# Sliding-window attention and a SwiGLU block on one core: two projection products trade places, two VectorE additions get precedence, and the last block's sums are held back

## The chip, the cores and the metric

The kernel runs on one core of a Trainium2 chip. The metric is device time in microseconds (us), the median of several runs; the kernel before takes 342.95 us (4 runs, 342.94 to 343.35). The core's engines work side by side and each takes its own instructions in a fixed order: TensorE (PE; its weight loads are listed as PEld), VectorE (DVE), ScalarE (ACT), GpSimd (POOL) and SyncE (SP). POOL, SP and ACT also issue transfers (DMA). An engine waits for another through semaphores.

## What is computed

The reference, cut to what matters:

```python
# attention: 8 batches, 8 heads, 576 tokens, head size 64, window 128, ALiBi bias
scores = scale * np.matmul(q, k.transpose(0, 1, 3, 2))
scores = np.where(mask, scores + bias[None], -1000000000.0)
attn = np.exp(scores - max); attn = attn / sum
x = (attn @ v) as 4608 tokens x 512
# SwiGLU block: d_model 512, d_ff 1536
g = x @ w_gate
silu = g * (1.0 / (1.0 + np.exp(-g)))
val = x @ w_val
out = (silu * val) @ w_out          # 4608 x 512, float32
```

## The kernel before

**Tiling.** The 4608 tokens are 9 blocks of 512 (n = 0 to 8). Attention is done in 36 units that produce `xT`, the transposed input of a block. The two wide products (gate and value) of a block produce `hT[n]`, 12 row tiles of 128 x 512. The last product (projection with `wo_sb`) turns `hT[n]` into output rows. The gate, value and projection work of one block runs beside the attention of later blocks and the projection of the block before: the code is generators, and `ffn()` and `everything()` decide which one is advanced next.

**The projection in seven products.** From block 1 on, the projection of a block is Strassen's scheme in Winograd's form: `strassen(n, t)` (line 507) runs for t = 0 and t = 1, each in seven steps of six 128x256 matmuls. Each step ends with a `yield`. X and Y are the two accumulators in PSUM. In the code's order the steps are:

1. X = A11 B11; ACT copies X (`p1s`) or, for blocks 5 to 7, seeds `p2` with it (lines 543 to 547)
2. p2 += A12 B21; DVE writes the top left output (`osb`, line 551 or 540)
3. X += S2 T2 (the "sixth" product); ACT copies X to `u2s` (line 558)
4. Y = S1 T1 (the "fifth" product); ACT copies Y to `p5s` (line 564), or DVE does for the last block's t = 1 (line 562)
5. X += S3 T3; DVE writes low right = X + `p5s` (line 540 through `half_plus`)
6. Y += S4 B22; DVE writes top right = Y + `u2s` (line 540)
7. X += A22 T4; low left (line 577 on DVE for the last block, else 579 on ACT)

For all blocks but the last, X and Y are halves of one PSUM tile, that is of one bank. For the last block (`end`) they are two tiles of the pool `ps_a`, two banks. S1 is made in place in `hT`, S2, S3 and S4 in three buffers, by four DVE instructions for every two row tiles (`four_sums`): S3 (line 488), S1 (489), S2 (490), S4 (491). S2 needs S1, S4 needs S2.

**Gate and value of the last three blocks in seven products.** For n = 6, 7 and 8 `gate_val_by_seven(n)` (line 615) does the gate and value products of a pair of row tiles u (0 to 5) in seven steps of four 128x256 matmuls, `first` to `seventh`. `third` adds on DVE v1 = Y + u2 (line 663) and multiplies it into `hT` (664); `seventh` adds v2 = X + p5 (line 670); `fourth` accumulates into X, which v2 has read, and its result goes through ACT (678) and DVE (679) into `hT`. `seven_steps()` interleaves two pairs: first(u), seventh(u-1), fifth(u), sixth(u), fourth(u-1), second(u), third(u), so that step number k of a block is 7u plus the place in this list. After every third step one step of `strassen(n-1, ...)` is put in.

**What sets the order.** From step 60 of the main loop on (which takes in all steps of the Strassen projection), PE's instructions stand in the order in which the code issues them (`manual_schedule` for PE alone). DVE and ACT instructions, ACT's transfers among them, are placed by the scheduler, by its own estimate of when they are ready and by their priority; `tc.high_priority()` raises the latter. Small DVE instructions that are not due yet are collected in `later`, and one or two of them are issued after a step.

**The end.** Block 8 has nothing after it. Step 1 of t = 0 is put in at k = 41; behind the last gate and value product come the other 13 steps of both halves, in the order t = 1, 0, 1, 0, 0, 0, 1, 0, 0, 1, 1, 1, 1 (line 780). So the steps at the end are, as t.step: 0.1, 1.1, 0.2, 1.2, 0.3, 0.4, 0.5, 1.3, 0.6, 0.7, 1.4, 1.5, 1.6, 1.7. The last block's outputs are stored in pieces by SP and ACT (`store(..., two)`, line 446).

Of the kernel before, what the change touches and what calls it, by code (L numbers as in the profile page):

```python
# [51 lines left out]
def kernel(  # L52
# [10 lines left out]
    nc = tc.nc  # L63
# [6 lines left out]
    NBLK = NTOK // 512  # L70
# [396 lines left out]
    T1, T2, T3, T4 = (consts.tile([P, HM, HC], FP16, name=f"T{n}") for n in (1, 2, 3, 4))  # L467
# [25 lines left out]
    def at_once(fs):  # L493
        for f in fs:
            f()
# [11 lines left out]
    def strassen(n, t):  # L507

        h = hT[n]
        A11, A12 = h[:, 0:HM, 0:256], h[:, HM:NMB, 0:256]  # L510
        S1, A22 = h[:, 0:HM, 256:512], h[:, HM:NMB, 256:512]
        S2, S3, S4 = hsum[n]
        cols = slice(t * P, (t + 1) * P)
        end = n == NBLK - 1
        seeded = SEVEN_FROM <= n + 1 < NBLK
        factor = 1.0 if n >= SEVEN_FROM else 0.5
        if end:
            X, Y = (ps_a.tile([P, HC], FP32, name="po", tag="a", bufs=4) for _ in range(2))
            p2 = ps_f.tile([P, HC], FP32, name="p2", tag="gv")
        else:  # L520
            po = ps_f.tile([P, 2, HC], FP32, name="po", tag="po", bufs=1)
            X, Y = po[:, 0, :], po[:, 1, :]
            p2 = (ps_f.tile([P, HC], FP32, name="p2", tag="gv") if seeded
                  else ps_a.tile([P, HC], FP32, name="p2", tag="a"))
        top, low = (opool.tile([P, DM], FP32, name="osb", tag="osb") for _ in range(2))
        if end and t:
            spare = [opool.tile([P, DM], FP32, name="osb", tag="osb") for _ in range(2)]
            p1s, p5s, u2s = spare[0][:, 0:HC], spare[0][:, HC:DM], spare[1][:, 0:HC]
        else:
            p1s, p5s, u2s = (supool.tile([P, HC], FP32, name=i, tag=i, bufs=1)  # L530
                             for i in ("p1s", "p5s", "u2s"))

        def product(dst, a, b, start=False):
            for m in range(HM):
                nc.tensor.matmul(dst, a[:, m, cols], b[:, m, :], start=(start and m == 0),  # L535
                                 stop=(m == HM - 1), skip_group_check=True)

        def half_plus(dst, a, b):
            with tc.high_priority() if n + 1 < SEVEN_FROM else ExitStack():
                nc.vector.scalar_tensor_tensor(out=dst, in0=a, scalar=factor, in1=b,  # L540
                                               op0=ALU.mult, op1=ALU.add)

        product(X, A11, B11, True)
        if seeded:
            nc.scalar.copy(p2, X)
        else:
            nc.scalar.mul(p1s, X, factor)
        yield
        product(p2, A12, B21, not seeded)
        if seeded:  # L550
            nc.vector.tensor_scalar_mul(top[:, 0:HC], p2, factor)
        else:
            half_plus(top[:, 0:HC], p2, p1s)
        if end and t:
            store(n, t, top, 0, HC)
        yield
        product(X, S2, T2)
        nc.scalar.mul(u2s, X, factor)
        yield
        product(Y, S1, T1, end)  # L560
        if end and t:
            nc.vector.tensor_scalar_mul(p5s, Y, factor)
        else:
            nc.scalar.mul(p5s, Y, factor)
        yield
        product(X, S3, T3)
        half_plus(low[:, HC:DM], X, p5s)
        if end and t:
            store(n, t + 2, low, HC, DM, True)
        yield  # L570
        product(Y, S4, B22)
        half_plus(top[:, HC:DM], Y, u2s)
        store(n, t, top, HC if end and t else 0, DM, end)
        yield
        product(X, A22, T4)
        if end:
            nc.vector.tensor_scalar_mul(low[:, 0:HC], X, factor)
        else:
            nc.scalar.mul(low[:, 0:HC], X, factor)
        store(n, t + 2, low, 0, HC if end and t else DM, end)  # L580
        yield
# [33 lines left out]
    def gate_val_by_seven(n):  # L615

        x = xT[n]
        A11, A12 = x[:, 0:HK, 0:256], x[:, HK:NKB, 0:256]
        S1, A22 = x[:, 0:HK, 256:512], x[:, HK:NKB, 256:512]
        S2, S3, S4 = xsum.pop(n)  # L620
        hT[n] = hpool.tile([P, NMB, 512], FP16, name="hT", tag="hT")
        live = {}

        def product(dst, w, c0, a, start=False):
            for i in range(2):
                for kb in range(HK):
                    nc.tensor.matmul(dst[:, i, :], w[:, kb, c0 + i * P:c0 + (i + 1) * P], a[:, kb, :],  # L627
                                     start=(start and i == 0 and kb == 0),
                                     stop=(i == 1 and kb == HK - 1), skip_group_check=True)

        def first(u):
            X, Y = (ps_a.tile([P, 2, 256], FP32, name=i, tag="a", bufs=4) for i in ("gX", "gY"))
            Z = ps_f.tile([P, 2, 256], FP32, name="gZ", tag="gv")
            live[u] = X, Y, Z
            product(X, G1, 2 * u * P, A11, True)
            nc.scalar.copy(Z, X)

        def fifth(u):
            Y = live[u][1]
            product(Y, tsum[u][0], 0, S1, True)  # L640
            p5 = epool.tile([P, 2, 256], FP32, name="p5", tag="exc", bufs=5)
            nc.scalar.copy(p5, Y)
            live[u] += (p5,)

        def second(u):
            Z = live[u][2]
            product(Z, G2, 2 * u * P, A12)
            s = supool.tile([P, 2, 256], FP16, name="s1", tag="tt")
            nc.scalar.activation(s, Z, AF.Silu)
            live[u] += (s,)  # L650

        def sixth(u):
            X = live[u][0]
            product(X, tsum[u][1], 0, S2)
            u2 = epool.tile([P, 2, 256], FP32, name="u2", tag="exc", bufs=5)
            nc.scalar.copy(u2, X)
            live[u] += (u2,)

        def third(u):
            X, Y, Z, p5, u2, s = live[u][:6]  # L660
            product(Y, V2, 2 * u * P, S4)
            v_ = supool.tile([P, 2, 256], FP16, name="v1", tag="uu")
            nc.vector.tensor_add(v_, Y, u2)
            nc.vector.tensor_mul(hT[n][:, 2 * u:2 * u + 2, 0:256], s, v_)

        def seventh(u):
            X, Y, Z, p5, u2, s = live[u]
            product(X, tsum[u][2], 0, S3)
            v_ = supool.tile([P, 2, 256], FP16, name="v2", tag="uu")
            nc.vector.tensor_add(v_, X, p5)  # L670
            live[u] += (v_,)

        def fourth(u):
            X, v_ = live[u][0], live[u][-1]
            del live[u]
            product(X, tsum[u][3], 0, A22)
            s = supool.tile([P, 2, 256], FP16, name="s2", tag="tt")
            nc.scalar.activation(s, X, AF.Silu)  # L678
            nc.vector.tensor_mul(hT[n][:, 2 * u:2 * u + 2, 256:512], s, v_)  # L679

        return {f.__name__: f for f in (first, second, third, fourth, fifth, sixth, seventh)}
# [23 lines left out]
    def ffn():  # L705
# [44 lines left out]
        for n, k, name, which in seven_steps():  # L750
            if k == 0 and n > SEVEN_FROM:
                assert next(parts, 0) == 0
                parts = chain(strassen(n - 1, 0), strassen(n - 1, 1))
            if n == SEVEN_FROM and k in (1, 3, 10, 17):
                later.extend(gate_val_weight_sums(2 + (k + 4) // 7))
            yield 0.5
            if k % 3 == 2 and k < 42:
                next(parts)
                yield 0.75
            if k == 20 and n + 1 < NBLK:  # L760
                later.extend(x_sums(n + 1))
            if k == 35:
                later.extend(sums(n, 0))
            if name == "fourth" and which is not None and which[1] > 3:
                if which == (NBLK - 1, 5):
                    at_once(final)
                else:
                    later.extend(sums(which[0], which[1] - 3))
            if n == NBLK - 1 and k == 40:
                final = sums(n, 2)  # L770
                later.append(final.pop(0))
            for _ in range(2 if len(later) > 4 or k >= 39 or k < 7 else 1):
                if later:
                    later.pop(0)()
            if n == NBLK - 1 and k == 41:
                next(ends[0])
                yield 0.75
# [235 lines left out]
```

The softmax here doesn't subtract the row's maximum and nothing guards it: scores larger than these inputs give would overflow.

## Time and profile before

| | |
|---|---|
| median of 4 runs | 342.95 us |
| the profiled execution's own time | 343.14 us |
| its span, first to last instruction | 341.3 us |
| PE busy / DVE / ACT | 329.8 / 277.3 / 207.0 us |
| mean granted TensorE clock | 0.998 |

DVE's busy time by stretch (the windows view, 40 us each): 34.6 us in 40 to 80, 33.3 in 80 to 120, 36.0 in 120 to 160, 37.9 in 160 to 200, 39.9 in 200 to 240; then 12.9 in 240 to 260, 15.7 in 260 to 280 and 13.8 in 280 to 300 (20 us each). Blocks 6 to 8 with their seven products begin at about 244 us; the last gate and value product ends at about 327.8 us, the last matmul at about 337.1 us.

How to read a line of the timeline: start, duration, engine, line of the kernel, operation, output tile <- input tiles, size, count of merged instructions, and in brackets the idle time before it with what ended it. The tile names are the program's without buffer numbers: `po` is X or Y of the projection, `T` is one of T1 to T4, `S` one of S2 to S4, and `po<-T,hT` is a product with S1 or A22, which lie in `hT`. A PE row's duration holds the passage through the array; from the start of one 128x256 matmul to the next it is 0.109 us.

### The profile page before, as it was taken

How to read it: one execution, taken by the hardware profiler on the slowest of the kernel's cores; microseconds unless marked ns; L12 is line 12 of the kernel's file. 1: busy time of each engine (PE TensorE's matmuls, PEld its weight loads, DVE VectorE, ACT ScalarE, POOL GpSimd, SP SyncE). 2: the span in 40 equal slices, each digit the busy share in tenths (PEclk: the TensorE clock that was granted, in tenths of full speed). 3: DMA queues.
4: the chain of work that ended last, by engine and by line, in shares of the span. 5: the costliest groups of instructions: out<-in, count | busy, mean ns of one | idle time of the engine just before them, and what ended most of it. 6: DMA issues, size and time to landing. Idle time of an engine off the chain costs nothing.

```text
span 341.3 us, 7787 instructions
## 1 busy us (share of the span) xinstructions
PE 329.8 (97%) x2983; PEld 218.5 (64%) x2983; DVE 277.3 (81%) x652; ACT 207.0 (61%) x412; POOL 109.6 (32%) x136
## 2 busy tenths in 40 slices
PE   7999989999999999999999999999999999999994
PEld 4484445444456566566655655665788878888884
DVE  6577886999798779998899999999855975775683
ACT  3758676465766675656655557463477667676640
POOL 8968672548865175834017000000000000000000
PEclk9999999999999999999999999999999999999999
DMA  9999999899999999999969922041101101011014
GB/s 154 170 180 175 164 170 151 79 140 160 160 172 140 172 155 158 164 158 140 200 130 101 179 33 79 15 85 27 61 16 48 63 0 64 24 40 63 0 71 116
DMA packets 160037, 37.37 MB, mean 109 GB/s; under 512 B 147328, under 2 KB 155648, under 8 KB 160000
## 3 DMA queue, kind: packets, MB, share of 16 engines
q0 software_dynamic: 118336, 18.62, 82.3%
q1 hardware_dynamic: 40976, 17.64, 28.7%
q10 hardware_dynamic: 688, 0.62, 0.6%
q8 instruction: 23, 0.38, 0.5%
q14 instruction: 14, 0.11, 0.1%
HBM read 37.91 MB, written 9.44 MB: 139 GB/s over the span
## 4 chain that ended last, share of the span: by engine, by line
PE 75%; DVE 14%; ACT 6%; issue 2%; DMA 1%; ACTq 0%; DVEq 0%
PE po L535 16%; PE pg L400 14%; PE pv L400 14%; PE gX L627 8%; PE av L348 4%; PE gY L627 4%; PE ps L280 3%; PE po L454 2%; PE p L535 2%; DVE hT L430 2%; PE gZ L627 2%; ACT tt L418 2%; ACT ex L286 2%; DVE uu L419 2%; PE px L374 1%
## 5 line engine op out<-in xcount | busy, mean ns | idle before, releaser
L400 PE MATMUL pv<-xT,wv_sb 128*128 128x512 f16 (+2 forms) x320 | 76.5, 358 | 0.6 <-DVE uu L419 0.3
L400 PE MATMUL pg<-xT,wg_sb 128*128 128x512 f16 (+2 forms) x320 | 75.8, 358 | 0.3 <-DVE xT L376 0.2
L418 ACT ACTIVATE tt<-pg 128x512 f16<-128x512 f32 (+2 forms) x70 | 41.3, 590 | 47.7 <-PE pg L400 46.6
L286 ACT ACTIVATE ex<-ps 128x512 f16<-128x512 f32 x96 | 50.0, 606 | 9.9 <-PE ps L280 9.9
L419 DVE SCALAR_TENSOR_TENSOR uu<-tt,pg 128x512 f16<-128x512 f16 (+2 forms) x69 | 46.0, 667 | 10.5 <-ACT tt L418 10.2
L430 DVE TENSOR_TENSOR hT<-uu,pv 128x512 f16<-128x512 f16 (+2 forms) x70 | 46.7, 667 | 3.0 <-PE pv L400 1.3
L185 POOL DMA_DIRECT2D va<-in_v_dram x40 | 34.4, 863 | 36.9 <-PE av L348 28.8
L400 PEld LDWEIGHTS <-wv_sb 128*128 128x128 f16 x320 | 28.3, 98 | 25.1 <-issue 3.2
L535 PEld LDWEIGHTS <-hT 128*128 128x128 f16 x384 | 37.0, 98 | 10.6 <-issue 0.8
L400 PEld LDWEIGHTS <-wg_sb 128*128 128x128 f16 x320 | 28.2, 98 | 23.3 <-issue 2.6
L191 POOL DMA_DIRECT2D kn<-in_k_dram x39 | 33.3, 858 | 19.8 <-DMA kT<-kn 10.7
L191 POOL DMA_DIRECT2D qn<-in_q_dram x39 | 33.5, 865 | 16.0 <-DMA va<-in_v_dram 8.2
L535 PEld LDWEIGHTS <-S 128*128 128x128 f16 x288 | 27.3, 98 | 9.0 <-issue 1.4
L292 DVE TENSOR_TENSOR ex<-ex,m_reg 128x1024 f16<-128x1024 f16 x42 | 28.8, 687 | 3.0 <-ACT ex L286 3.0
L351 DVE TENSOR_TENSOR x<-av,rec 128x256 f16<-128x256 f32 x72 | 28.8, 420 | 0.4
L535 PE MATMUL po<-T,S 128*128 128x256 f16 x192 | 26.5, 273 | 0.6 <-DVE S L490 0.3
L535 PE MATMUL po<-T,hT 128*128 128x256 f16 x192 | 26.0, 273 | 0.1
L679 DVE TENSOR_TENSOR hT<-s,v 128x512 f16<-128x512 f16 x18 | 7.6, 424 | 18.5 <-ACT s L678 18.5
L320 ACT ACTIVATE exc<-psc 128x512 f16<-128x512 f32 x40 | 21.3, 609 | 1.9 <-PE psc L316 1.9
L348 PEld LDWEIGHTS <-ex 128*128 128x128 f16 x384 | 17.4, 97 | 4.6 <-issue 1.3
L348 PE MATMUL av<-va,ex 128*128 128x65 f16 x384 | 19.3, 193 | 0.7 <-ACT ex L286 0.7
L280 PE MATMUL ps<-qT,kT 64*128 64x256 f16 x192 | 16.7, 272 | 0.4 <-DVE qT L223 0.2
(134 smaller groups left out, 537.5 us busy)
## 6 DMA issues: line engine op xcount, KB each, us to landing
out_dram<-osb SPq DMA_DIRECT2D x32, 256.0 KB, 2.5
va<-in_v_dram POOLq DMA_DIRECT2D x32, 128.0 KB, 7.9
qn<-in_q_dram POOLq DMA_DIRECT2D x31, 128.0 KB, 8.7
kn<-in_k_dram POOLq DMA_DIRECT2D x31, 128.0 KB, 8.1
wg_sb<-in_moe_w_gate_dram POOLq DMA_DIRECT2D x6, 256.0 KB, 7.6
wv_sb<-in_moe_w_val_dram POOLq DMA_DIRECT2D x6, 256.0 KB, 8.1
wo_sb<-in_moe_w_out_dram POOLq DMA_DIRECT2D x2, 768.0 KB, 9.3
kn<-in_k_dram POOLq DMA_DIRECT2D x8, 64.0 KB, 7.4
```

Source lines behind the costliest of these rows:

```text
L185: nc.gpsimd.dma_start(va[rank][p0:p1, :, 0:D], src)
L191: nc.gpsimd.dma_start(t_[p0:p1], src)
L286: nc.scalar.activation(e[:, o:o + 2, :], banks[q4][par], AF.Exp, scale=scale)
L292: nc.vector.tensor_mul(e[:, o, :], e[:, o, :], reg[:, o, :])
L348: nc.tensor.matmul(av[:, j, :], w, val, start=(n == 0), stop=(n == len(todo) - 1))
L351: nc.vector.tensor_mul(x[:, 4 * half:4 * half + 4, :], av[:, :, 0:D], rec.broadcast_to([P, 4, D]))
L400: nc.tensor.matmul(ps[:, c0:c1], w[:, kb, ms], xT[n][:, kb, c0:c1], start=(kb == 0 and c0 == 0), stop=(kb == NKB - 1 and c1 == 512), skip_ ...
L418: nc.scalar.activation(tt, pg[:, c0:c1], AF.Tanh, scale=0.5)
L419: nc.vector.scalar_tensor_tensor(out=uu, in0=tt, scalar=one if (n, m) == PIN else 1.0, in1=pg[:, c0:c1], op0=ALU.add, op1=ALU.mult)
L430: nc.vector.tensor_mul(hT[n][:, m, c0:c1], acted[(n, m)][1][:, c0:c1], pv[:, c0:c1])
L535: nc.tensor.matmul(dst, a[:, m, cols], b[:, m, :], start=(start and m == 0), stop=(m == HM - 1), skip_group_check=True)
L627: nc.tensor.matmul(dst[:, i, :], w[:, kb, c0 + i * P:c0 + (i + 1) * P], a[:, kb, :], start=(start and i == 0 and kb == 0), stop=(i == 1 an ...
```

## The change

1. In `strassen`, the steps 3 and 4 trade places: first Y = S1 T1 with `p5s`, then X += S2 T2 with `u2s`. The order of t at the end (line 780) stays.
2. In `third` and `seventh` of the gate and value products, the additions v1 and v2 are issued with high priority.
3. In `ffn`, the single instruction of the last sums (S3 of block 8's last pair), which is appended to `later` at k = 40, isn't taken out at k = 40 and 41, nor is what else lies in `later`; at the last `fourth` all that is left in `later` is issued ahead of `final`.

```diff
@@ strassen(n, t)
-        product(X, S2, T2)
-        nc.scalar.mul(u2s, X, factor)
-        yield
         product(Y, S1, T1, end)
         if end and t:
             nc.vector.tensor_scalar_mul(p5s, Y, factor)
         else:
             nc.scalar.mul(p5s, Y, factor)
+        yield
+        product(X, S2, T2)
+        nc.scalar.mul(u2s, X, factor)
         yield
         product(X, S3, T3)
@@ gate_val_by_seven(n)
         def third(u):
...
-            nc.vector.tensor_add(v_, Y, u2)
+            with tc.high_priority():
+                nc.vector.tensor_add(v_, Y, u2)
...
         def seventh(u):
...
-            nc.vector.tensor_add(v_, X, p5)
+            with tc.high_priority():
+                nc.vector.tensor_add(v_, X, p5)
@@ ffn()
                 if which == (NBLK - 1, 5):
-                    at_once(final)
+                    at_once(later + final)
+                    later.clear()
...
             for _ in range(2 if len(later) > 4 or k >= 39 or k < 7 else 1):
-                if later:
+                if later and (n + 1 < NBLK or k not in (40, 41)):
                     later.pop(0)()
```

In the built program, the two kernels' instructions differ in these places only. On PE the products with S1 and with S2 stand in each other's place, in all 16 halves. On ACT `u2s` and `p5s` trade places, except at the very end: there the order `u2s` (t = 0), `p5s` (t = 0), `u2s` (t = 1), store, store becomes `p5s` (t = 0), `u2s` (t = 0), store of the top half, store of the low half, `u2s` (t = 1). On DVE, in the first pair of block 7 and of block 8, the order S2, v1, S4, hT, v2 becomes v1, S2, v2, S4, hT; at the end `p5s` (t = 1) moves ahead of two output instructions. SP's and POOL's orders are the same, and so is the place of every sum of block 8 on DVE.

## The prediction

> **What bounds the kernel now.** I read the page's busy lines first, then the waits of PE, then the timeline around each wait.
>
> ```profile
> PE 329.8 (97%) x2983; PEld 218.5 (64%) x2983; DVE 277.3 (81%) x652; ACT 207.0 (61%) x412; POOL 109.6 (32%) x136
> ...
> PEclk9999999999999999999999999999999999999999
> ```
>
> PE is busy for 97% of the span at full granted clock, and the change neither adds nor removes a matmul. So a gain can only come out of PE's idle time, and a loss is new idle time on PE or a longer way behind its last matmul. The waits of PE over the whole span, those that bear on the change:
>
> ```profile
> PE gX L627 <- DVE v L670: 0.9, 2, 0.6
> ...
> PE po L535 <- DVE S L490: 0.3, 1, 0.3
> ...
> PE p L535 <- DVE hT L664: 0.3, 1, 0.3
> PE po L535 <- ACT p5s L564: 0.3, 1, 0.3
> ```
>
> Two waits on v2 (line 670) and one on S2 (line 490) are what parts 1 and 2 can reach. The reader is to see how little there is: about 1.2 us in the column of totals. A wait is listed without the passage through the array, so what it costs I take from start to start of the matmuls (0.109 us each when nothing waits).
>
> **Part 2, precedence for v1 and v2.** The timeline at block 7's first pair:
>
> ```profile
> 274.90 0.42 DVE L551 TENSOR_SCALAR osb<-p 128x256 f32<-128x256 f32 x1
> 275.24 0.41 DVE L490 TENSOR_TENSOR S<-hT 128x512 f16<-128x512 f16 x1
> 275.57 0.69 DVE L663 TENSOR_TENSOR v<-gY,u 128x512 f16<-128x512 f32 x1
> 276.17 0.42 DVE L491 TENSOR_TENSOR S<-hT,S 128x512 f16<-128x512 f16 x1
> 276.50 0.42 DVE L664 TENSOR_TENSOR hT<-s,v 128x512 f16<-128x512 f16 x1
> 276.83 0.69 DVE L670 TENSOR_TENSOR v<-gX,p 128x512 f16<-128x512 f32 x1
> ```
>
> ```profile
> 275.17 0.93 PE L535 MATMUL po<-T,S 128*128 128x256 f16 x6
> 275.94 0.60 PE L627 MATMUL gY<-xT,kT 128*128 128x256 f16 x4
> 276.38 0.60 PE L627 MATMUL gX<-m_reg,kT 128*128 128x256 f16 x4
> 277.58 0.60 PE L627 MATMUL gX<-xT,kT 128*128 128x256 f16 x4 [0.60 <-DVE v L670]
> ```
>
> The last PE row, the fourth product, overwrites what v2 reads and starts 0.06 us after v2's end. In the new order v1, S2, v2, DVE starts v1 at 275.24, S2 0.60 later (a v's start to the next start) at 275.84, v2 0.33 later at 276.18; v2 ends at 276.87 and PE starts at 276.92 instead of 277.58: gain 0.66. Without any wait PE would come at 276.70 (the S2 product loses 0.11 at 275.7 in the same rows, which part 1 takes away; that is contained in the 0.66). Block 8's first pair is the same picture: the sixth product starts at 304.65, the fourth would follow at 305.08 and starts at 305.51. DVE's line 551 starts at 302.84; with v1 at 303.17, S2 at 303.78, v2 at 304.12, v2 ends at 304.81, before PE arrives: gain 0.43. What is pushed back is S4 and the `hT` product by at most 0.7 us; S4 is first read in step 6, over 5 us later, and the `hT` tile by sums of the next stage, so I cost that at nothing. Were it late, the S4 step would wait and the price is the same 0.7.
>
> **Part 1, before the end.** Step 3 waits for S2 once by more than 0.2 us, in block 3's projection:
>
> ```profile
> 139.74 0.42 DVE L489 TENSOR_TENSOR hT<-hT 128x512 f16<-128x512 f16 x1
> ...
> 141.01 0.42 DVE L490 TENSOR_TENSOR S<-hT 128x512 f16<-128x512 f16 x1
> ...
> 141.48 0.39 PE L535 MATMUL po<-T,S 128*128 128x256 f16 x2 [0.32 <-DVE S L490]
> ```
>
> The six matmuls start at 140.56 and the next product at 141.71, 1.15 us where 0.66 is needed: 0.49 lost. With S1's product here only line 489 must be done, at 140.16. Gain 0.49, if it lasts. Against that: DVE is full from 165 to 194 and from 199 to 244 us (37.9 and 39.9 of 40 us busy), and an engine that is itself the pace would keep PE waiting as much later on. For it: DVE is idle fourteen times by over 0.1 us from 143 to 165, and for 0.74 us at 198.9, mostly for ACT results that come from PE, so DVE moves forward with PE. Bounds 0 and 0.49; I take 0.49. In all other halves X and Y lie in one bank, so each step waits for ACT's copy of the step before it, in either order; that wait is the `p5s` line above, and it stays.
>
> **Part 1, at the end.** Here X and Y are two banks. Before, the order 0.3 (X), 0.4 (Y), 0.5 (X) hides `u2s` behind the Y product, and that of 1.3 (X) behind the three products up to 1.5 (X). Now 0.4 and 0.5 are both X with ACT's copy between them, and so are 1.4 and 1.5.
>
> ```profile
> 330.18 0.97 PE L535 MATMUL po<-T,S 128*128 128x256 f16 x6
> 330.99 0.82 PE L535 MATMUL po<-T,hT 128*128 128x256 f16 x6
> 331.19 0.38 ACT L558 ACTIVATE u2s<-po 128x256 f32<-128x256 f32 x1 [2.17 <-PE po L535]
> 331.64 1.47 PE L535 MATMUL po<-T,S 128*128 128x256 f16 x12
> ```
>
> ACT starts 0.31 us after the start of a product's last matmul (330.88 to 331.19), takes 0.38, and PE follows 0.05 after (from the p5s wait at 107.50, where ACT ended at 107.45). New times, by the old clock: 0.3 at 330.18 (line 489 ends at 330.03), 0.4 at 330.83, its last matmul at 331.38, `u2s` 331.69 to 332.07, 0.5 at 332.12 instead of 331.64: loss 0.48, in which the old wait for S2 of 0.15 is made good. Then 1.3 at 332.78, 0.6 at 333.43, 0.7 at 334.09, 1.4 at 334.74, last matmul 335.29. ACT could copy `u2s` of t = 1 at 335.60. But two stores now stand ahead of it on ACT. The first waits for DVE's top half (step 0.6: 334.29 to 334.71), the second for the low half (step 0.7: 334.94 to 335.37). How long an issue holds ACT, the old end shows:
>
> ```profile
> 334.26 0.56 ACTq L446 DMA_DIRECT2D out_dram<-osb  x1
> ...
> 334.92 0.73 ACTq L446 DMA_DIRECT2D out_dram<-osb  x1
> ```
>
> These are the same two stores. The first runs 334.74 to 335.30, the second 335.40 to 336.13; `u2s` 336.17 to 336.55, and 1.5 starts at 336.60 instead of 334.92: in all 1.69 later. From there to the last landing all follows as before. That an ACT instruction behind an issue waits for its end, one place shows: the table load at 1.65 us starts 0.03 after the issue at 1.17 that took 0.45. By that the price of the second pair is 1.21; its bounds are 0.63 (copy alone) and 1.55 (an issue of 1.07 us, the longest of ACT's five at the end, at 337.71, in the place of the second).
>
> The Trainium skill's page DMA: Bandwidth & Descriptors, section Issuing engines are not separate DMA queues, says that the issuing sequencer's time is usually small beside the transfer. Taken as nothing, `u2s` would start at 335.60 and the sum be 0.58 lower; the rows with 0.56 and 0.73 us speak against it here. The page PSUM — Partial Sum Buffer (its table of what to do) advises to read one bank while the matmuls write another; the old order at the end did this, the new one doesn't, and no rule there gives the wait a price.
>
> **Part 3** adds nothing: DVE's order at the end has every sum where it was.
>
> **The sum**, against the profiled 343.14 us with its span of 341.34: gains 0.66 + 0.43 + 0.49 = 1.58, losses 0.48 + 1.21 = 1.69, together +0.11: span 341.45. The same on the median of 342.95: 343.06. About 0.2% (0.69 us) is what can be told from no change.
>
> **Rivals.**
> - *ACT is not held by the issues.* For it: the copy needs no part of the transfer's data. Against it: ACT's last issue, ready at 337.53, started at 337.71, after the one before had ended at 337.62. The loss becomes 0.48 + 0.63: 342.48.
> - *The early gain at 141 is lost again* in the stretch where DVE is full. 343.06 + 0.49 = 343.55.
> - *Slower: the issues on ACT decide the end.* The place is the two stores ahead of `u2s` (t = 1). ACT's five issues took 0.50 to 1.07 us. With 1.07 for both, the first ends at 335.81, the second at 336.91, 1.5 starts at 337.38: 0.78 more, 343.84. It is slower by over 0.2% once the two take 0.58 more than the 1.30 in the sum. Against it: the same two stores took 0.56 and 0.73 beside SP's.
> - *Faster: the waits at the end cost little*, for instance because the scheduler's or PE's waits are met earlier than I place them. If both copies cost nothing, the end gains its 0.15 and the time is 342.95 - 1.58 - 0.15 = 341.2; against it stands that accumulation into X and ACT's read of X can't overlap.
> - *The change doesn't do what it says.* Part 3 is that case; for parts 1 and 2 the built order shows the move.
>
> **Chances.** Forecast 0.50, ACT not held 0.15, early gain lost 0.14, slower 0.11, faster 0.10. A third of the lost-gain case goes over the line to slower (other issue times add to it), and of ACT not held a fifth falls under 342.26: faster 0.13, same 0.71, slower 0.16. The likeliest is 343.05. The range reaches from the case in which ACT isn't held (342.48, less 0.07 for a small wait of S2 products that I left out) to the slower one: 342.4 to 343.85.
>
> **What would show it.** PE's fourth product of the first pairs of blocks 7 and 8 with at most 0.2 us of wait left; no wait for S2 near 141 us and the products after 245 us earlier by about 0.5; two new waits `po` <- ACT `u2s` (line 564) at the end, the second about twice the first, with ACT's two issues ahead of its copy; the distance from step 0.3 to the last matmul longer by 1.7 us. I am wrong if the products between 245 and 270 us aren't earlier, if the second of the new waits is no longer than the first, or if any half other than the last two shows a new wait.

## The result, and the profile after

The changed kernel is slower by a little: the ratio of its runs to those of the kernel before is 1.0015, with a 95% interval of 1.001 to 1.002. The medians are 343.71 us (30 runs) and 343.24 us (48 runs). So it moved by +0.5 us, less than the 0.2% that the prediction called the line to no change, and in the direction in which its sum pointed (+0.11).

The page of the changed kernel, the lines that answer to those shown before:

```profile
PE 329.2 (96%) x2983; PEld 218.5 (64%) x2983; DVE 277.3 (81%) x652; ACT 206.9 (61%) x412; POOL 109.6 (32%) x136
...
PEclk9999999999999999999999999999999999999999
```

The busy times agree within 0.6 us and PE's granted clock is full in both pages; what changed is where PE stands still. The waits of PE after 90 us (engine, line, what ended the wait: us in total, times, longest):

```profile
PE po L535 <- ACT osb L564: 1.1, 1, 1.1
PE po L535 <- ACT u2s L564: 0.7, 2, 0.5
PE av L348 <- ACT ex L286: 0.7, 2, 0.5
PE p L535 <- DVE hT L665: 0.3, 1, 0.3
```

The two waits on v2 (0.9 us) and the one on S2 (0.3 us) are gone from the list, and two waits on ACT's `u2s` stand in their place: one of 0.5 us (the other of the two in the second line is the old one at 107 us, which was named after `p5s` before) and one of 1.1 us, where ACT writes `u2s` of t = 1 into a tile named `osb`.

**Blocks 7 and 8.** The timeline of DVE and of PE at block 7's first pair:

```profile
275.20 0.68 DVE L664 TENSOR_TENSOR v<-gY,u 128x512 f16<-128x512 f32 x1
275.80 0.42 DVE L490 TENSOR_TENSOR S<-hT 128x512 f16<-128x512 f16 x1
276.13 0.68 DVE L672 TENSOR_TENSOR v<-gX,p 128x512 f16<-128x512 f32 x1
```

```profile
275.14 0.82 PE L535 MATMUL po<-T,hT 128*128 128x256 f16 x6
275.79 0.60 PE L627 MATMUL gY<-xT,kT 128*128 128x256 f16 x4
276.23 0.60 PE L627 MATMUL gX<-m_reg,kT 128*128 128x256 f16 x4
276.87 0.60 PE L627 MATMUL gX<-xT,kT 128*128 128x256 f16 x4
```

From the start of step 3 (275.14) to that of the fourth product it is 1.73 us where it was 2.41 (275.17 to 277.58). The trace has 0.67 less, with 0.21 of wait left; the forecast had 0.66 and 0.22. At block 8's first pair no wait is left. Its sixth and fourth products, first of the kernel before, then of the changed one:

```profile
304.65 0.60 PE L627 MATMUL gX<-m_reg,kT 128*128 128x256 f16 x4
305.51 0.60 PE L627 MATMUL gX<-xT,kT 128*128 128x256 f16 x4 [0.26 <-DVE v L670]
```

```profile
303.94 0.60 PE L627 MATMUL gX<-m_reg,kT 128*128 128x256 f16 x4
304.38 0.60 PE L627 MATMUL gX<-xT,kT 128*128 128x256 f16 x4
```

The distance of 0.86 us has become 0.44, the pace of four matmuls: 0.43 gained in the trace.

**The end.** PE's and ACT's timelines:

```profile
329.71 0.82 PE L535 MATMUL po<-T,S 128*128 128x256 f16 x6
331.00 0.82 PE L535 MATMUL po<-T,S 128*128 128x256 f16 x6 [0.47 <-ACT u2s L564]
...
333.61 0.82 PE L535 MATMUL po<-T,S 128*128 128x256 f16 x6
335.55 0.81 PE L535 MATMUL po<-T,S 128*128 128x256 f16 x6 [1.12 <-ACT osb L564]
```

```profile
333.69 0.56 ACTq L446 DMA_DIRECT2D out_dram<-osb  x1
...
334.35 0.73 ACTq L446 DMA_DIRECT2D out_dram<-osb  x1
...
335.12 0.38 ACT L564 ACTIVATE osb<-po 128x256 f32<-128x256 f32 x1 [4.17 <-PE po L535]
```

Start to start, a product of six takes 0.655 us. The distance 329.71 to 331.00 is 0.63 more, that from 333.61 to 335.55 is 1.29 more. ACT was idle for 4.17 us and `u2s` of t = 1 had its input at about 334.5 (0.31 us after the last matmul's start at 334.16), but it started at 335.12, 0.05 after the second store's issue had ended.

**Near 142 us** the wait for S2 is gone, but little of it is gained. PE and DVE, first of the kernel before, then of the changed one:

```profile
141.94 1.03 PE L400 MATMUL pv<-xT,wv_sb 128*128 128x512 f16 x4
142.89 0.61 PE L280 MATMUL ps<-qT,kT 64*128 64x256 f16 x8
...
142.16 0.76 DVE L351 TENSOR_TENSOR x<-av,rec 128x256 f16<-128x256 f32 x2
```

```profile
141.56 1.03 PE L400 MATMUL pv<-xT,wv_sb 128*128 128x512 f16 x4
142.52 0.96 PE L280 MATMUL ps<-qT,kT 64*128 64x256 f16 x8
...
142.28 0.76 DVE L351 TENSOR_TENSOR x<-av,rec 128x256 f16<-128x256 f32 x2
```

The eight score matmuls take 0.96 us where they took 0.61. They write into PSUM buffers of the pool that `av` also comes from, and these are still read by the two `x<-av` instructions of DVE (line 351), which end at 142.70 and 143.03, and 0.06 us after each a score matmul starts that stood waiting (142.76 and 143.09). In the kernel before they end at 142.58 and 142.91, and PE, which starts the eight at 142.89, is held up by neither. DVE's work in between is the same and lies where it did (all of it 0.12 us later in this execution, from the first 100 us on).

**A measure without the start.** The executions differ in their first 100 us by chance: the first product with one of T1 to T4 (the first `po<-T` row) starts at 102.29 to 103.06 us in the thirteen profiles of this case. So the runs below are compared by the distance from there to the start of the last matmul, called the way of PE: 234.49 us before, 235.01 in the changed kernel, +0.52.

### The profile page after: what moved, and what is told of

It reads as the page before. It is cut to its first block, busy times and chain, and to the rows that moved or that the text cites. A ratio compares the mean times of both kernels' runs of the same rounds, so it can differ in the third digit from the quotient of the medians.

```text
span 341.7 us, 7782 instructions
## 1 busy us (share of the span) xinstructions
PE 329.2 (96%) x2983; PEld 218.5 (64%) x2983; DVE 277.3 (81%) x652; ACT 206.9 (61%) x412; POOL 109.6 (32%) x136
## 4 chain that ended last, share of the span: by engine, by line
PE 65%; DVE 20%; POOL 4%; ACT 3%; issue 3%; DMA 3%; ACTq 0%; DVEq 0%; POOLq 0%
PE po L535 14%; PE pg L400 12%; PE pv L400 11%; PE gX L627 8%; PE gY L627 4%; DVE hT L430 3%; DVE uu L419 3%; PE av L348 3%; DMA qn<-in_q_dram 3%; PE ps L280 3%; PE p L535 2%; PE gZ L627 2%; DVE x L351 2%; DVE ex L292 2%; PE po L454 2%
```

## Experiments

Ratios are to the kernel before on the same chip. The way of PE and the landing of the last store come from one profile of each run. The part of the change that holds back the last sums was not run alone: built with it alone, the program has the same instructions in the same order on every engine as the kernel before.

| run | median, before beside it | ratio, 95% interval | way of PE | last landing after the last matmul's start |
|---|---|---|---|---|
| kernel before | | | 234.49 | 3.44 |
| e0_changed_again | 343.76, 343.37 | 1.0012 (1.0003 to 1.0021) | 235.01 | 3.18 |
| e1_swap_only | 344.63, 343.02 | 1.0046 (1.0033 to 1.0059) | 236.02 | 3.27 |
| e2_precedence_only | 342.77, 343.02 | 0.9989 (0.9979 to 1.0000) | 234.10 | 3.27 |
| e3_old_order_at_end | 341.96, 343.02 | 0.9968 (0.9956 to 0.9980) | 233.18 | 3.29 |
| e4_interleaved_end | 342.13, 343.02 | 0.9971 (0.9960 to 0.9982) | 233.03 | 3.65 |
| e5_no_issue_on_act | 342.73, 343.37 | 0.9983 (0.9974 to 0.9992) | 234.37 | 3.06 |
| e6_release_bank_first | 343.53, 343.37 | 1.0009 (1.0000 to 1.0018) | 234.68 | 3.53 |
| e10_best | 341.87, 343.37 | 0.9959 (0.9945 to 0.9973) | 232.90 | 3.20 |
| e8_interleaved_and_bank | 341.53, 343.06 | 0.9956 (0.9944 to 0.9969) | 232.71 | 3.46 |
| e12_one_store_less_on_act | 341.69, 343.06 | 0.9961 (0.9948 to 0.9973) | 232.71 | 3.77 |
| e10_best_again | 342.07, 343.06 | 0.9961 (0.9947 to 0.9975) | 232.86 | 3.34 |

### The parts alone

`e1_swap_only` is the kernel before with the first hunk of the change, `e2_precedence_only` with the second.

> Part 1 alone (the products with S1 and S2 trade places in all halves, no precedence, sums not held back). Theory (the end decides): PE loses about 1.77 us at the end through the two waits for u2s, as in the profile of the changed kernel (0.63 and 1.29, less the old wait for S2 of 0.14), gains 0.15 near 141 us, and gains nothing in the first pairs of blocks 7 and 8, where v2 still comes last: about +1.5 us against the kernel before. Rival (the end costs little, the loss lies elsewhere): within 0.3 us of the kernel before.

> Part 2 alone (v1 and v2 with high priority, the old order of products). Theory (part 2 needs part 1): S2 now ends 0.6 us later while step 3 still waits for it, so PE loses 0.69 at block 7 and 0.26 at block 8 on S2 and wins only 0.18 + 0.17 on v2: -0.35 us against the kernel before, with two waits po <- S (line 490) in place of those on v2. Rival (the parts add up): 0.66 + 0.43 less the 0.11 for S2, about -1.0 us.

The swap alone: the way of PE is 1.53 us longer, as the theory had it. Its waits from 110 us on:

```profile
PE po L535 <- ACT osb L564: 1.1, 1, 1.1
PE gX L627 <- DVE v L670: 1.0, 2, 0.7
PE po L535 <- ACT u2s L564: 0.5, 1, 0.5
PE p L535 <- DVE hT L664: 0.3, 1, 0.3
```

The waits on v2 are still there (1.0 where it was 0.9): S2 no longer stops PE in these pairs, and PE waits longer for v2. The precedence alone shortens the way by 0.39 (expected 0.35, and 1.0 by the rival):

```profile
PE po L535 <- DVE S L490: 0.8, 2, 0.5
PE p L535 <- DVE hT L665: 0.3, 1, 0.3
```

Here the waits on v2 are gone, and PE waits for S2 instead. (The list has the idle time without the passage through the array and leaves out the smallest; start to start S2 costs 0.48 us at 141.8, 0.69 at 276.6 and 0.25 at 304.4.) So the two parts do not add up: alone they give +1.53 and -0.39, which sum to 1.14, and together they give +0.52. The swap takes S2 out of PE's way, and only then is v1's and v2's precedence worth 0.43 + 0.66 us instead of 0.39.

### The end put back

```diff
@@ e3_old_order_at_end: strassen(n, t) of the changed kernel
+        for f in (sixth_step, fifth_step) if end else (fifth_step, sixth_step):
+            f()
+            yield
@@ e4_interleaved_end: ffn() of the changed kernel
-        for t in (1, 0, 1, 0, 0, 0, 1, 0, 0, 1, 1, 1, 1):
+        for t in (1, 0, 1, 0, 0, 1, 0, 1, 0, 0, 1, 1, 1):
```

> The changed kernel with the old order of steps 3 and 4 in the last block alone. Theory (the loss is the end's): -0.15 near 141 us, -0.66 and -0.43 at blocks 7 and 8, the end as in the kernel before: -1.2 us against it, about -1.7 against the changed kernel, and no wait of PE for u2s at the end. Rival (something else in the change costs time too): less than 0.8 us faster than the kernel before.

> The changed kernel with another order of the two halves at the end: t = 1, 0, 1, 0, 0, 1, 0, 1, 0, 0, 1, 1, 1, so that a product into another accumulator stands between the product with S2 and the one with S3 in both halves. Theory: neither u2s is waited for, nor S2: from step 0.3 to the last matmul 5.9 us without a wait instead of 7.8 to 8.4: -1.9 us against the changed kernel, -1.4 against the kernel before (0.15 better than with the old order at the end). Rival (another wait, p5s on DVE or the stores, takes the place): no better than e3.

With the old order in the last block alone the way of PE is 1.31 us shorter than before and 1.83 shorter than in the changed kernel; from 110 us on one wait is listed, the old one for the last `hT`:

```profile
PE p L535 <- DVE hT L670: 0.3, 1, 0.3
```

That settles where the loss lies: the changed kernel is slower only for its last 8 us. The interleaved order is 0.15 us better still on PE, exactly the wait for S2 at the end that it avoids, but the median shows nothing of it (342.13 against 341.96, with overlapping intervals): in the profile the last store lands 3.65 us after the last matmul's start instead of 3.29. ACT's last issue, first in e3, then in e4:

```profile
336.39 0.92 ACTq L446 DMA_DIRECT2D out_dram<-osb  x1
```

```profile
335.20 0.56 ACTq L446 DMA_DIRECT2D out_dram<-osb  x1
...
335.85 0.56 ACTq L446 DMA_DIRECT2D out_dram<-osb  x1
...
336.50 0.78 ACTq L446 DMA_DIRECT2D out_dram<-osb  x1
```

In e4 the products are so close together that ACT's issues stand nearly one behind the other. That explains little of the 0.36, though: the last issue begins 0.24 us after its data are there (DVE's last instruction ends at 336.26), and in e3 it is 0.18. The other 0.3 us lies between the start of the issue and the landing, 2.67 us in e4 and 2.38 in e3. In the other profiles whose last landing is one of ACT's, this time is 2.27 to 2.62, the longest of them in e6, whose end has the changed kernel's order. So how much of it comes from the closer order and how much from chance is not shown.

### What holds `u2s`

```diff
@@ e5_no_issue_on_act: strassen(n, t) of the changed kernel
-        store(n, t, top, HC if end and t else 0, DM, end)
+        store(n, t, top, HC if end and t else 0, DM, bool(end and t))
...
-        store(n, t + 2, low, 0, HC if end and t else DM, end)
+        store(n, t + 2, low, 0, HC if end and t else DM, bool(end and t))
```

> The changed kernel once more, so that the next runs can be compared with it on one chip: +0.4 to +0.6 us against the kernel before, the second wait for u2s at the end 1.29 us from start to start of the matmuls beyond their pace.

> The changed kernel with both pieces of the last block's t = 0 stores issued by SP, so that ACT has no issue ahead of u2s of t = 1. Theory (the issues hold ACT): the second wait falls from 1.29 to 0.63 us, the first stays at 0.63, and the time falls by 0.65 us against the changed kernel. Rival (the wait is the copy and its dependences, not the issues): the second wait stays over 1.1 us and the time within 0.2 us.

PE's and ACT's timelines of e5:

```profile
333.72 0.82 PE L535 MATMUL po<-T,S 128*128 128x256 f16 x6
335.00 0.81 PE L535 MATMUL po<-T,S 128*128 128x256 f16 x6 [0.47 <-ACT osb L564]
```

```profile
334.57 0.38 ACT L564 ACTIVATE osb<-po 128x256 f32<-128x256 f32 x1 [3.52 <-PE po L535]
```

The repeat e0 came out as expected (+0.39 us in the medians, +0.52 in the way of PE, the second wait 1.29). In e5 ACT starts the copy 0.31 us after the start of the product's last matmul, as it does where nothing holds it. The second wait is 0.63 us, like the first, and the way of PE is 0.64 shorter than in e0. The median fell by 1.0 us (ratio 0.9983 against 1.0012; by the two intervals at least about 0.4), the landing being 0.12 us shorter too and the rest within what the intervals leave. So the issue of a store on ACT does hold the copy that stands behind it; the rival in which it doesn't has fallen.

### What took back the early gain

```diff
@@ e6_release_bank_first: weighted(i) of the changed kernel
+            with tc.high_priority() if i == 20 else ExitStack():
                 nc.vector.reciprocal(rec, av[:, :, D:D + 1])
                 nc.vector.tensor_mul(x[:, 4 * half:4 * half + 4, :], av[:, :, 0:D],
                                      rec.broadcast_to([P, 4, D]))
```

> The changed kernel with the normalising of one attention unit (the reciprocals and multiplications of unit 20, lines 350 and 351, near 142 us) at high priority, so that DVE does it ahead of S2 and of a mask product. Theory (the early gain was taken back by the wait for the PSUM bank that these instructions release, 0.34 us of the 0.49): that stall goes, and PE is 0.3 us earlier from there to the end: -0.3 us against the changed kernel. Rival (DVE as a whole is the pace there, another wait takes the place): less than 0.1 us.

In e6 DVE does `x<-av` ahead of S2 (its line numbers are one higher here):

```profile
141.76 0.76 DVE L352 TENSOR_TENSOR x<-av,rec 128x256 f16<-128x256 f32 x2
142.44 0.41 DVE L491 TENSOR_TENSOR S<-hT 128x512 f16<-128x512 f16 x1
...
142.94 0.61 PE L280 MATMUL ps<-qT,kT 64*128 64x256 f16 x8
```

The score matmuls take 0.61 us again, and the way of PE is 0.33 shorter than in the changed kernel: the gain lasts to the end, through the stretch in which DVE is full. The medians differ by 0.23 us in the same direction, but their intervals overlap, so it is the trace that shows this.

### Better than the kernel before and the changed one

> The old order of steps 3 and 4 in the last block and the priority for unit 20 together: if both theories hold, 0.3 us under the version with the old order at the end alone, that is -1.35 us against the kernel before (0.996); if the rival of the unit 20 run holds, no better than that version (0.9968).

> The version with the old order at the end and the priority for unit 20 once more, on the same chip as e8 and e12: 0.996 of the kernel before, last landing 3.3 to 3.45 us after the start of the last matmul.

> The interleaved order at the end (as in e4) with the priority for unit 20 (as in e6). In e4 the last matmul came 0.15 us earlier by its own clock than with the old order, but the last store landed 3.65 us after it instead of 3.29 to 3.44, because ACT issued four stores back to back. Theory: the same here, so the time is within 0.2 us of e10 and about -1.3 us against the kernel before. Rival (e4's longer landing was chance): 0.2 to 0.3 us faster than e10.

> As e8, with both pieces of the low half of t = 0 issued by SP, so that ACT has four issues at the end in place of five. Theory (the time of the issues on ACT bounds the end of e4 and e8): the last landing moves to 3.2 to 3.4 us after the start of the last matmul, 0.3 us faster than e8. Rival (SP's issues become as late): no difference over 0.1 us, with SP's last issue now the late one.

e10 is e3 with e6's priority: 0.9959 and 0.9961 of the kernel before, 0.3% under the plain precedence (e2). Its way of PE is 1.6 us shorter than before. e8 (e4 with the priority) has the shortest way, 232.71, with a landing of 3.46. Its median lies 0.5 us under e10's beside it, where 0.2 at most was expected, but the intervals overlap, and the start of e10's profile was 0.76 us later; whether e8 is better than e10 stays open. e12 missed its theory: with one store less on ACT its median is 0.16 us above e8's, not 0.3 below, at the same way of PE. As its rival had it, SP's last issue is now the late one, and the landing is 3.77. So ACT's issues alone do not bound the end of e8.

## Why the prediction held, and what in it was off

The measured median, 343.71 us, lies 0.65 above the forecast's 343.06. Of that, 0.29 is the level of the kernel before, whose median over the 48 runs was 343.24; the rest is mainly one term of the sum, the early gain. The result is nearer to the rival in which the early gain is lost again (343.55) than to the forecast, also when 0.29 is added to both. That the small +0.11 had the right sign is partly luck, as that one term had bounds 0.49 apart. Of the signs named in advance one came in part only: the products between 245 and 270 us are earlier by 0.15 us, counted from the first `po<-T` row, and not by about 0.5.

Point by point, by the prediction's own steps:

- **Part 2: -0.66 and -0.43.** Measured the same to 0.01 us (0.67 and 0.43), with 0.21 of wait left at block 7. That these sums hold only with part 1 in place was in the 0.11 for S2, but not said; e2 shows it.
- **Part 1 before the end: -0.49, bounds 0 and 0.49.** This is the term that was mis-sized: 0.15 came through. The wait for S2 did go, and the rival "lost again" named the right reason, DVE as the pace, but the wrong place and time: not in the full stretch from 165 us on, but 1.6 us behind, at the next thing that PE needs from the same DVE queue. I argued from DVE's idle time after 143 us that DVE would move forward with PE; but from 138 us on the first idle time over 0.03 us in the kernel before is at 143.8, so nothing ahead of that could move forward. e6 confirms the place.
- **Part 1 at the end: +0.48 and +1.21, together 1.69.** Measured 1.77 from step 0.3 to step 1.5. Of the two waits the first is exact (0.63), the second 1.29 instead of 1.21: DVE's top half (step 0.6) now waits for PE and for ACT and started 0.38 us after the last matmul's start where I had put 0.31, and both issues and the copy moved back by that 0.07. The issues took 0.56 and 0.73 us again, so the rival in which they decide the end (both 1.07) did not happen; nor did the one in which ACT is not held, as the second wait was 1.29 and not 0.63, and e5 shows why.
- **"From there to the last landing all follows as before."** It was 3.23 us instead of 3.44 in the profile, 0.21 less: ACT's last issue took 0.87 us instead of 1.07.
- **Part 3: nothing.** The built order says so; it was not run alone. The other terms leave 0.01 us of the way of PE for it.

With the measured terms the sum is -0.66 - 0.43 - 0.15 + 1.77 = +0.53 for the way of PE (measured +0.52), +0.12 by chance at the start and -0.21 behind the last matmul: +0.44, against a span of 341.7 instead of 341.3.

Of the two pages of the Trainium skill that the prediction weighed: DMA: Bandwidth & Descriptors (Issuing engines are not separate DMA queues) calls the time that it takes to initiate a transfer usually small beside the transfer. In the changed kernel ACT's five issues at the end took 0.50 to 0.87 us of the 2.3 to 3.0 us to the landing, 22 to 38%, and on an engine that also computes it cost 0.64 us of PE's time (e5). PSUM — Partial Sum Buffer (Summary: rules for kernel authors) advises to read another bank than the one that a running matmul writes. The orders that do so at the end, e3 and e4, have a way of PE that is 1.83 and 1.98 us shorter than the changed kernel's.

## What to carry to other kernels

When a wait of a busy engine on another busy engine is removed, look for the next thing that it needs from that same queue. Here the releasing engine had no idle time in between, so 0.34 of the 0.49 us was lost there, and a change in that engine's order brought it back (e6). An edit can be worth more behind another one than alone (precedence for v1 and v2: 0.39 us alone, 1.09 with S2 out of the way), so price each with and without the other. Where nothing follows, as at this program's end, products into one accumulator need another product between the write and the next write for the copy to hide behind (0.63 us each time without one), and a transfer's issue that stands ahead of that copy on a computing engine's queue counts as work of that engine (0.64 us more).

## What the runs showed of the hardware that was not expected

- The same two stores issued by ACT took 0.56 and 0.73 us in the kernel before and in the changed one, though at other times and with other neighbours; where the stores come closely together (e4) ACT's five took 0.56 to 0.78.
- The first 100 us vary from execution to execution by up to 0.76 us (102.29 to 103.06, before rounding), more than most of the effects here. In the changed kernel's profile PE waited for input transfers twice in the first 30 us (0.7 and 0.6 us), in the profile of before for none. From there on the same matmuls keep their distances to about 0.05 us (232.90 and 232.86 in the two profiles of e10; 235.01 twice in the changed kernel).
